# An attention and gMLP block on one core: the order written out for the first loads, batch 0 and the last two output tiles

## The chip, the cores and the metric

The kernel runs on one core of one Trainium2 chip. The metric is the time of one execution on the device in microseconds; the median of three runs is given. The profile is of one execution, and its times are microseconds from the first instruction.

## The reference

Sliding-window attention with sink positions is followed by a gMLP block. Four batches, eight heads, 768 positions, head width 64; the eight heads side by side give the 512 columns of `x`.

```python
scores = scale * q @ k.T                       # scale = 1/8
keep = (pos_k < 4) | (0 <= pos_q - pos_k < 128)
a = softmax(where(keep, scores, -1e9))
x = (a @ v).transpose(0, 2, 1, 3).reshape(4, 768, 512)
h = gelu_tanh(x @ w_in)                        # 512 -> 1024
u, v = h[..., :512], h[..., 512:]
v_n = (v - mean(v)) / sqrt(var(v) + 1e-6) * g_ln
v_s = w_sg @ v_n + b_sg[:, None]               # over the 768 positions
out = x + (u * v_s) @ w_out                    # 512 -> 512
```

All inputs and the output are float32.

## The kernel before

The whole program is a list of steps written out by hand, `STEPS` (lines 20 to 68). A step is a function's name and its indices: `QK.0.2.1` calls `QK(0, 2, 1)`. The loop at line 650 calls them in this order, and nothing reorders them, so the list fixes the order on each engine's queue. An engine takes its own instructions strictly in that order and waits for each until its inputs are there and its output buffer is free. A last letter in a step names the engine: D is VectorE (DVE), A is ScalarE (ACT), P is GpSimd (POOL).

The names, in the order of the data (b is the batch, p a pair of heads, g a group of two tiles of 128 positions, t one such tile):

- `LPK.g`, `LPQ.g` (lines 239 to 247): loads of k and q of batch 0, one pair of heads in each, issued by SyncE (SP) in float32. `CPK`, `CPQ` cast them to bfloat16. `LG` loads `g_ln`, `LC` the four sink rows of v.
- `LK`, `LQ`, `LVH`, `LW`, `LWS`, `LWO` (lines 213 to 280): loads that GpSimd issues and that cast on the way: k and q of batches 1 to 3, v by halves of the heads, `w_in` by column halves (`LW.0` is the half for v, `LW.1` for u), `w_sg` by halves and `w_out`.
- `TK`, `TQ`, `EK`, `EQ`: transposes of k and q on TensorE (PE) and the copies out of PSUM. In batch 0, `TK.0.p` transposes one pair of heads with all positions; in batches 1 and 2, `TQ.b.g` takes two tiles of all heads. Batch 3 uses transposing DMAs from SP instead: `DK`, `DQ`, and `XD` for x in batches 2 and 3.
- `QK.b.p.g` (line 463): scores of a pair of heads for two tiles, into one of two PSUM buffers `sc`. With a last `.1` it first adds a mask bias by two matmuls with the identity (lines 466 to 468). `EX` is the exponential on ScalarE, `MK` sets masked entries to zero where QK had no bias: one multiply on VectorE, or two selects on GpSimd.
- `KS`, `SK`, `SX`: the same for the sink positions. `VSK`, `VSO`, `VSM` prepare the sink rows of v.
- `AV.b.p.k` (line 502) multiplies with v, `NR` divides by the row sums and writes x.
- `XT`, `XE` transpose x on TensorE. `MV`, `GV` give the v half of gelu(x w_in), `BN`, `RS`, `NM`, `Z` its normalisation; `MU`, `GU` the u half. `WT`, `WE` transpose w_sg.
- `SP` (the step, not the engine SP), `GT`, `GM`: the product over positions, the scale and bias, the product with u.
- `OU.b.t`, `RA.b.t`, `ST.b.t` (lines 630 to 641): the last product for one tile of 128 positions, four matmuls of 512 columns into a PSUM buffer `mm`; one add of x on VectorE into a buffer `ot`; one store of 256 KB by SP.
- `HM.n` puts n matmuls on zeros ahead of the next buffer that TensorE writes (line 188), `WARM` clears their operand.

Buffers are taken in turn: four PSUM buffers `mm`, two `sc`, ten `P`, six `ot`. A step that takes the next one waits until its last reader is done; for `ot` that is the store of six tiles earlier.

While batch b is in its gMLP part, batch b+1 is in its attention part, and the list weaves the two together. Only at the start (batch 0's attention) and at the end (batch 3's gMLP) does one batch run alone.

Of the kernel before, what the change touches and what calls it, by code (L numbers as in the profile page):

```python
# [17 lines left out]


STEPS = """  # L20
WARM LPK.0 FILL LPQ.0 LPK.1 LG LPQ.1 LPK.2 MASK LPQ.2 LPK.3 CPK.0.A IDEN LPQ.3 IDEN2 MASK0 HM.8 TK.0.0 CPQ.0.A
EK.0.0.A HM.1 TQ.0.0 CPK.1.D EQ.0.0.A ZERO HM.1 TK.0.1 LC CPQ.1.P QK.0.0.0.1 EK.0.1.A QK.0.0.1 LVH.0.0 EX.0.0.0
CPK.2.D TQ.0.1 EX.0.0.1 GTR EQ.0.1.D TK.0.2 QK.0.0.2 LVH.0.1 CPQ.2.A GCP.D EK.0.2.D QK.0.1.0.1 EX.0.0.2 TQ.0.2 CPK.3.D
LQ.1.0 EX.0.1.0 CPQ.3.D QK.0.1.1 TK.0.3 EQ.0.2.D EX.0.1.1 MK.0.0.1.P TQ.0.3 EK.0.3.D QK.0.1.2.1 EQ.0.3.A VSK LQ.1.1
VSO QK.0.2.0.1 EX.0.1.2 KS.0 VSM.0 SK.0.1 LW.0 MK.0.1.1.D AV.0.0.0 SX.0.1 AV.0.1.0 EX.0.2.0 QK.0.2.1 LWS.0 NR.0.0.0
AV.0.0.1 EX.0.2.1 NR.0.1.0 AV.0.1.1 LW.1 QK.0.3.0.1 NR.0.0.1 LQ.1.2 QK.0.3.1.1 MK.0.2.1.D EX.0.3.0 NR.0.1.1 MK.0.0.2.P
AV.0.2.0 EX.0.3.1 AV.0.2.1 NR.0.2.0 AV.0.3.0 SK.0.2 NR.0.2.1 QK.0.2.2 SX.0.2 QK.0.3.2 NR.0.3.0 EX.0.2.2 AV.0.3.1
AV.0.0.2 NR.0.3.1 AV.0.1.2 EX.0.3.2 MK.0.2.2.P XT.0.0 NR.0.0.2 XT.0.1 NR.0.1.2 XE.0.0.A TQ.1.0 LK.1.0 AV.0.2.2
XE.0.1.A EQ.1.0.D MV.0.0 MK.0.3.2.P NR.0.2.2 LQ.1.3 AV.0.3.2 GV.0.0 MV.0.1 LK.1.1 NR.0.3.2 BN.0.0 LWS.1 XT.0.2 LK.1.2
# [46 lines left out]
def kernel(  # L76
# [14 lines left out]
    nc = tc.nc  # L91
# [4 lines left out]
    d_model = H * Dh  # L96
# [7 lines left out]
    KU = d_half // 128  # L104
# [26 lines left out]
    mm_ring = Ring("mm", 4, [128, 512], F32, psum)  # L131
# [6 lines left out]
    x_sb = Ring("x_sb", 2, [128, NT, d_model], BF16)  # L138
# [5 lines left out]
    ot = Ring("ot", 6, [128, d_model], F32)  # L144
# [21 lines left out]
    w_out_sb = sb.tile([128, KU, d_model], BF16, name="w_out_sb")  # L166
# [10 lines left out]
    def gated(b, hf):  # L177
        return gatedT[:, slots.setdefault((b, hf), len(slots) % 3)]
# [458 lines left out]
    def RA(b, t):  # L637
        nc.vector.tensor_add(ot.new((b, t)), mm_ring["o", b, t], x_sb[b][:, t, :])  # L638
# [51 lines left out]
```

## Time and profile before

| What | Value |
|---|---|
| median of the runs shown | 157.92 us (157.89, 157.92, 160.23) |
| the profiled execution | 159.1 us, its span 157.4 us |
| TensorE matmul busy | 147.8 us |
| VectorE busy | 126.7 us |
| ScalarE busy | 98.2 us |
| GpSimd busy | 97.1 us |
| last add ends, last store is issued | 154.3 us |

The span goes from the first to the last instruction. The profiled execution takes 1.7 us more than its span, and the runs without a profile are the ones that the median is taken of. Busy times of different engines overlap. A matmul's record covers its way through the array, so matmuls that follow each other overlap in the records; the distance between their starts is what each costs: 0.216 us for 512 columns, 0.109 us for 256. DMA issues of GpSimd take its queue's time, 0.9 us for a 128 KB load and 1.4 to 1.8 us for half of v.

### The profile page before, as it was taken

How to read it: one execution, taken by the hardware profiler on the slowest of the kernel's cores; microseconds unless marked ns; L12 is line 12 of the kernel's file. 1: busy time of each engine (PE TensorE's matmuls, PEld its weight loads, DVE VectorE, ACT ScalarE, POOL GpSimd, SP SyncE). 2: the span in 40 equal slices, each digit the busy share in tenths (PEclk: the TensorE clock that was granted, in tenths of full speed). 3: DMA queues.
4: the chain of work that ended last, by engine and by line, in shares of the span. 5: the costliest groups of instructions: out<-in, count | busy, mean ns of one | idle time of the engine just before them, and what ended most of it. 6: DMA issues, size and time to landing. Idle time of an engine off the chain costs nothing.

```text
span 157.4 us, 3863 instructions
## 1 busy us (share of the span) xinstructions
PE 147.8 (94%) x1554; PEld 95.5 (61%) x1567; DVE 126.7 (81%) x301; ACT 98.2 (62%) x108; POOL 97.1 (62%) x123
## 2 busy tenths in 40 slices
PE   6779799999998999999999999999999999999990
PEld 2355567679755759658366766457566644786540
DVE  5149986899989989497999995589999958947991
ACT  3769889548995884857986857356897013690000
POOL 3069959999969999997637916904359720302300
PEclk9978999999999999999999999999999999999998
DMA  5989999999999996999999286899000577610055
GB/s 168 314 319 112 147 202 208 167 189 215 157 150 181 154 147 45 133 139 145 144 153 187 42 223 158 226 222 142 4 0 0 104 174 298 228 71 2 0 193 209
DMA packets 83034, 23.88 MB, mean 152 GB/s; under 512 B 75524, under 2 KB 79880, under 8 KB 83016
## 3 DMA queue, kind: packets, MB, share of 16 engines
q0 software_dynamic: 64608, 11.01, 94.9%
q1 hardware_dynamic: 18408, 12.62, 28.5%
q8 instruction: 12, 0.20, 0.5%
q14 instruction: 6, 0.05, 0.1%
HBM read 24.81 MB, written 6.29 MB: 198 GB/s over the span
## 4 chain that ended last, share of the span: by engine, by line
PE 73%; DVE 12%; DMA 9%; issue 1%; SPq 1%; POOL 0%; DVEq 0%
PE mm L617 17%; PE sc L597 13%; PE sc L556 13%; PE mm L634 12%; DMA v_sb<-in_v_dram 5%; PE sc L473 5%; DMA uT<-in_q_dram 4%; DVE P L485 3%; PE mm L514 3%; DVE x_sb L531 3%; DVE gtmp L622 3%; PE mm L374 3%; PE mm L518 2%; PE mm L540 2%; PE mm L521 2%
## 5 line engine op out<-in xcount | busy, mean ns | idle before, releaser
L478 ACT ACTIVATE P<-sc 128x1024 bf16<-128x1024 f32 (+1 forms) x48 | 43.4, 953 | 9.6 <-PE sc L473 9.4
L617 PE MATMUL mm<-wsgT,z 128*128 128x384 bf16 x192 | 34.2, 326 | 0.2 <-DVE x_sb L531 0.2
L617 PEld LDWEIGHTS <-z 128*128 128x128 bf16 x192 | 17.9, 98 | 11.3 <-issue 0.4
L488 POOL TENSOR_SCALAR_AFFINE_SELECT P<-P 128x512 bf16<-128x512 bf16 x20 | 14.6, 729 | 16.5 <-ACT P L478 12.3
L560 ACT ACTIVATE vt<-sc 128x1024 f32<-128x1024 f32 x12 | 12.3, 1024 | 20.0 <-PE sc L556 20.0
L622 DVE SCALAR_TENSOR_TENSOR gtmp<-mm,g_sb,b_bc 128x384 bf16<-128x384 f32 x32 | 18.9, 609 | 4.8 <-PE mm L617 4.8
L634 PE MATMUL mm<-w_out_sb,wsg_gated 128*128 128x512 bf16 x88 | 21.9, 379 | 0.6 <-DVE x_sb L531 0.2
L627 POOL TENSOR_TENSOR wsg_gated<-gtmp,uT 128x384 bf16<-128x384 bf16 x14 | 13.2, 957 | 14.9 <-DVE gtmp L622 13.6
L597 PE MATMUL sc<-xT,w_in_sb 128*128 128x256 bf16 x192 | 22.3, 273 | 0.0
L556 PE MATMUL sc<-w_in_sb,xT 128*128 128x512 bf16 x93 | 22.1, 379 | 0.2
L569 DVE BATCH_NORM_STATS2 st<-vt 128x6 f32<-128x512 f32 x24 | 15.4, 684 | 6.5 <-ACT vt L560 6.5
L597 PEld LDWEIGHTS <-w_in_sb 128*128 128x128 bf16 x192 | 18.7, 98 | 3.1
L531 DVE TENSOR_TENSOR x_sb<-mm,rcp 128x384 bf16<-128x384 f32 (+1 forms) x36 | 18.5, 513 | 1.2
L638 DVE TENSOR_TENSOR ot<-mm,x_sb 128x512 f32<-128x512 f32 x24 | 15.8, 683 | 2.0 <-PE mm L634 1.9
L514 PE MATMUL mm<-v_sb,P 128*128 128x65 bf16 x192 | 16.7, 194 | 0.7 <-DMA v_sb<-in_v_dram 0.7
L220 POOL DMA_DIRECT2D q<-in_q_dram x18 | 16.6, 936 | 0.0
L514 PEld LDWEIGHTS <-P 128*128 128x128 bf16 x192 | 14.3, 98 | 3.3 <-issue 1.1
L473 PE MATMUL sc<-qT,kT 64*128 64x128 bf16 (+1 forms) x256 | 15.3, 245 | 0.9 <-DVE kT L198 0.6
L220 POOL DMA_DIRECT2D k<-in_k_dram x18 | 16.1, 901 | 0.0
L485 DVE TENSOR_TENSOR P<-P,mask 128x768 bf16<-128x768 bf16 (+1 forms) x22 | 15.7, 729 | 0.4 <-ACT P L478 0.4
L518 PE MATMUL mm<-v_sb,P 128*128 128x65 bf16 x160 | 15.8, 194 | 0.0
L602 ACT ACTIVATE uT<-sc 128x1024 bf16<-128x1024 f32 x12 | 12.3, 1021 | 5.6 <-PE sc L597 5.5
(89 smaller groups left out, 230.9 us busy)
## 6 DMA issues: line engine op xcount, KB each, us to landing
out_dram<-ot SPq DMA_DIRECT2D x24, 256.0 KB, 2.3
v_sb<-in_v_dram POOLq DMA_DIRECT2D x8, 384.0 KB, 8.0
q<-in_q_dram POOLq DMA_DIRECT2D x18, 128.0 KB, 5.6
k<-in_k_dram POOLq DMA_DIRECT2D x18, 128.0 KB, 5.3
wsg_gated<-in_moe_w_sg_dram POOLq DMA_DIRECT2D x2, 576.0 KB, 8.4
w_in_sb<-in_moe_w_in_dram POOLq DMA_DIRECT2D x2, 512.0 KB, 9.4
uT<-in_k_dram SPq DMA_DIRECT2D x2, 384.0 KB, 3.1
uT<-in_q_dram SPq DMA_DIRECT2D x2, 384.0 KB
```

The source lines that it names most:

```text
L220: return nc.gpsimd.dma_start(out=dst.rearrange("p (h d) -> p h d", h=H), in_=heads(src, b, i))
L473: nc.tensor.matmul(sc[:, hl, c:c + 128 * ni], at(kT, b)[rows, j, p, :], at(qT, b)[rows, i:i + ni, p, :], start=not biased, stop=(not biase ...
L478: nc.scalar.activation(out=P.new((b, p, g))[:, :, 0:w], in_=sc_ring[b, p, g][:, :, 0:w], func=AF.Exp, scale=scale)
L485: nc.vector.tensor_mul(pt[:, :, 0:w], pt[:, :, 0:w], m.unsqueeze(1).to_broadcast([128, 2, w]))
L514: nc.tensor.matmul(av[:, il, hl, :], pt[:, hl, c:c + 128], vb[:, h, i, :], start=first, stop=False)
L518: nc.tensor.matmul(av[:, il, hl, :], pt[:, hl, c:c + 128], vb[:, h, i - 1, :], start=False, stop=(i < 2 and il == n - 1 and hl == 1))
L531: nc.vector.tensor_mul(x_sb.get(b)[:, i0:i0 + n, 128 * p:128 * (p + 1)].rearrange("p t (h d) -> p t h d", h=2), av[:, :, :, 0:Dh], rcp[:, ...
L556: nc.tensor.matmul(hp[:, jl, :], xT[b][:, 2 * g + jl, c, :], w_in_sb[:, c, d_half:2 * d_half], start=(c == 0), stop=(c == KD - 1))
L597: nc.tensor.matmul(hp[:, dc // 2, 256 * (dc % 2):256 * (dc % 2 + 1)], w_in_sb[:, c, 128 * dc:128 * (dc + 1)], xT[b][:, 2 * g:2 * g + 2, c, :],
L617: nc.tensor.matmul(ps[:, 0:NH], z[b][:, si, 128 * dc:128 * (dc + 1)], wsgT[:, si, NH * hf:NH * (hf + 1)], start=(si == 0), stop=(si == NT ...
L622: nc.vector.scalar_tensor_tensor(out=gtmp.new((b, hf, dc)), in0=mm_ring["g", b, hf, dc][:, 0:NH], scalar=g_sb[:, dc:dc + 1], in1=b_bc[:, N ...
L634: nc.tensor.matmul(ps, gated(b, hf)[:, dc, 128 * tl:128 * (tl + 1)], w_out_sb[:, dc, :], start=(dc == 0), stop=(dc == KU - 1))
```

## The change

The list is written in a new order and some steps go to another engine. All loads, transposes and products of before are still there. In particular:

- SP issues `LPQ.2` ahead of `LG` and `LPK.2`, and `LPQ.3` ahead of `LPK.3`.
- In batch 0, all three `QK` of pair 0 come ahead of `TK.0.1`. `CPK.1` goes from VectorE to GpSimd, `CPQ.1` from GpSimd to VectorE, `CPQ.2` from ScalarE to VectorE; some `EK`, `EQ` change places between ScalarE and VectorE.
- Biased are now QK.0.0.1, 0.0.2, 0.2.0 and 0.2.1 (four); before they were 0.0.0, 0.1.0, 0.1.2, 0.2.0, 0.3.0 and 0.3.1 (six). There are two more MK for it. `HM` has 15 matmuls instead of 10.
- On GpSimd, `LW.0` and `LWS.0` come straight behind the two `LVH` of batch 0, ahead of `LQ.1.0` and `LQ.1.1`.
- From batch 0's gMLP on, steps of all kinds stand in a new order, among them the loads of later batches, and the stores `ST.0.*` and `ST.1.*` on SP's queue.
- `OU`, `RA` and `ST` of the tiles 5 and 2 of batch 3 are replaced by `OH`, `RH` and `SH`, each twice, for 256 columns each time. `OH` with h = 1 writes into the same PSUM buffer as h = 0. In the list, `OH.3.5.1` stands ahead of `RH.3.5.0`, and `OH.3.2.1` ahead of `RH.3.2.0`.

```diff
 STEPS = """
-WARM LPK.0 FILL LPQ.0 LPK.1 LG LPQ.1 LPK.2 MASK LPQ.2 LPK.3 CPK.0.A IDEN LPQ.3 IDEN2 MASK0 HM.8 TK.0.0 CPQ.0.A
-EK.0.0.A HM.1 TQ.0.0 CPK.1.D EQ.0.0.A ZERO HM.1 TK.0.1 LC CPQ.1.P QK.0.0.0.1 EK.0.1.A QK.0.0.1 LVH.0.0 EX.0.0.0
-CPK.2.D TQ.0.1 EX.0.0.1 GTR EQ.0.1.D TK.0.2 QK.0.0.2 LVH.0.1 CPQ.2.A GCP.D EK.0.2.D QK.0.1.0.1 EX.0.0.2 TQ.0.2 CPK.3.D
-LQ.1.0 EX.0.1.0 CPQ.3.D QK.0.1.1 TK.0.3 EQ.0.2.D EX.0.1.1 MK.0.0.1.P TQ.0.3 EK.0.3.D QK.0.1.2.1 EQ.0.3.A VSK LQ.1.1
-VSO QK.0.2.0.1 EX.0.1.2 KS.0 VSM.0 SK.0.1 LW.0 MK.0.1.1.D AV.0.0.0 SX.0.1 AV.0.1.0 EX.0.2.0 QK.0.2.1 LWS.0 NR.0.0.0
-AV.0.0.1 EX.0.2.1 NR.0.1.0 AV.0.1.1 LW.1 QK.0.3.0.1 NR.0.0.1 LQ.1.2 QK.0.3.1.1 MK.0.2.1.D EX.0.3.0 NR.0.1.1 MK.0.0.2.P
-AV.0.2.0 EX.0.3.1 AV.0.2.1 NR.0.2.0 AV.0.3.0 SK.0.2 NR.0.2.1 QK.0.2.2 SX.0.2 QK.0.3.2 NR.0.3.0 EX.0.2.2 AV.0.3.1
-AV.0.0.2 NR.0.3.1 AV.0.1.2 EX.0.3.2 MK.0.2.2.P XT.0.0 NR.0.0.2 XT.0.1 NR.0.1.2 XE.0.0.A TQ.1.0 LK.1.0 AV.0.2.2
-XE.0.1.A EQ.1.0.D MV.0.0 MK.0.3.2.P NR.0.2.2 LQ.1.3 AV.0.3.2 GV.0.0 MV.0.1 LK.1.1 NR.0.3.2 BN.0.0 LWS.1 XT.0.2 LK.1.2
-GV.0.1 WT.0 XE.0.2.D WT.1 LK.1.3 WT.2 VSM.1 MV.0.2 LQ.1.4 VSM.2 BN.0.1 LQ.1.5 MU.0.0 GV.0.2 LB.P BN.0.2 RS.0.1 MU.0.1
-GU.0.0 LQ.2.0 NM.0.1 WE.0.D WE.1.A RS.0.2 WE.2.D TK.1.0 GU.0.1 LQ.2.1 NM.0.2 MU.0.2 Z.0.0.D Z.0.1.D Z.0.4.A LK.1.4
-EK.1.0.D Z.0.5.D LK.1.5 TQ.1.1 GU.0.2 WT.3 EQ.1.1.D LK.2.0 WT.4 TK.1.1 KS.1 Z.0.2.D Z.0.3.A LVH.1.0 QK.1.0.0 WE.3.D
-QK.1.1.0 SP.0.0.0 EK.1.1.D WE.4.D SP.0.0.1 LK.2.1 EX.1.0.0 EX.1.1.0 MK.1.0.0.D LWO WT.5 TQ.1.2 GT.0.0.0 WE.5.A
-QK.1.0.1 MK.1.1.0.D QK.1.1.1 EX.1.0.1 GT.0.0.1 SP.0.0.2 GM.0.0.1.P EX.1.1.1 SP.0.0.3 GT.0.0.2 LVH.1.1 EQ.1.2.A
-GM.0.0.2.D QK.1.2.0 GT.0.0.3 QK.1.2.1 SP.0.1.0 EX.1.2.0 GM.0.0.3.D LK.2.2 GM.0.0.0.D EX.1.2.1 QK.1.3.0 GT.0.1.0 LK.2.3
-SK.1.0 EX.1.3.0 MK.1.1.1.D TK.1.2 LQ.2.2 SP.0.1.1 MK.1.2.0.D SX.1.0 EK.1.2.D GM.0.1.0.P TQ.2.0 GT.0.1.1 QK.1.0.2
-LQ.2.3 QK.1.3.1 MK.1.0.1.D EX.1.0.2 SP.0.1.2 MK.1.2.1.D LQ.3.0 EX.1.3.1 EQ.2.0.D AV.1.0.0 AV.1.1.0 MK.1.0.2.P GT.0.1.2
-TK.2.0 NR.1.0.0 QK.1.1.2 EK.2.0.A QK.1.2.2 LVH.3.0 AV.1.0.1 MK.1.3.0.D EX.1.1.2 NR.1.1.0 OU.0.0 NR.1.0.1 MK.1.3.1.P
-EX.1.2.2 OU.0.1 RA.0.0 QK.1.3.2 MK.1.1.2.P RA.0.1 QK.2.0.0 EX.1.3.2 AV.1.2.0 AV.1.3.0 NR.1.2.0 SP.0.1.3 MK.1.2.2.P
...
-QK.3.1.0 EX.3.0.0 AV.2.0.1 MK.2.2.2.P GT.1.1.1 XD.2.0 SP.1.1.2 EX.3.1.0 NR.2.0.1 AV.2.1.1 MK.3.1.0.D ST.0.0 GM.1.1.0.D
-QK.2.3.2 ST.0.1 GM.1.0.3.D QK.3.0.1 EX.2.3.2 ST.0.2 GT.1.1.2 AV.2.2.1 NR.2.1.1 OU.1.0 EX.3.0.1 MK.2.3.2.D SK.3.0
-NR.2.2.1 MK.3.0.1.P QK.3.2.0 AV.2.3.1 EX.3.2.0 SP.1.1.3 NR.2.3.1 SX.3.0 MU.2.0 XD.2.1 GT.1.1.3 RA.1.0 GM.1.1.3.P
-ST.1.0 OU.1.1 GM.1.1.2.P GU.2.0 OU.1.2 GM.1.1.1.P RA.1.1 MV.2.0 ST.1.1 LK.3.4 RA.1.2 ST.0.3 ST.0.4 MK.3.0.0.D LK.3.5
-ST.0.5 MK.3.2.0.D AV.3.0.0 LVH.3.1 GV.2.0 MV.2.1 BN.2.0 MV.2.2 GV.2.1 BN.2.1 MU.2.2 GV.2.2 BN.2.2 RS.2.1 MU.2.1 GU.2.2
...
-GT.3.1.2 OU.3.0 GM.3.1.2.P GT.3.1.3 OU.3.1 GM.3.1.3.D RA.3.0 OU.3.3 RA.3.1 ST.3.0 OU.3.4 ST.3.1 RA.3.3 OU.3.5 ST.3.3
-RA.3.4 OU.3.2 ST.3.4 RA.3.5 ST.3.5 RA.3.2 ST.3.2
+WARM LPK.0 FILL LPQ.0 IDEN LPK.1 LPQ.1 LPQ.2 LG IDEN2 MASK LPK.2 LPQ.3 CPK.0.A MASK0 LPK.3 HM.8 TK.0.0 CPQ.0.A
+EK.0.0.D HM.1 TQ.0.0 ZERO EQ.0.0.A HM.3 QK.0.0.0 CPK.1.P QK.0.0.1.1 EX.0.0.0 LVH.0.0 EX.0.0.1 MK.0.0.0.D QK.0.0.2.1
+CPQ.1.D TK.0.1 EX.0.0.2 LC CPQ.2.D VSK TQ.0.1 LVH.0.1 EK.0.1.D TQ.0.2 EQ.0.1.A EQ.0.2.A HM.1 QK.0.1.0 LW.0 QK.0.1.1
+CPQ.3.D EX.0.1.0 LWS.0 CPK.2.D EX.0.1.1 HM.2 TQ.0.3 CPK.3.D LQ.1.0 TK.0.2 EQ.0.3.D TK.0.3 EK.0.2.A LQ.1.1 QK.0.1.2
+EK.0.3.D GTR EX.0.1.2 QK.0.2.0.1 VSO KS.0 VSM.0 EX.0.2.0 SK.0.2 MK.0.1.2.P SK.0.1 MK.0.1.0.D QK.0.3.0 GCP.A AV.0.0.0
+EX.0.3.0 AV.0.1.0 NR.0.0.0 LW.1 QK.0.2.1.1 SX.0.1 MK.0.3.0.D SX.0.2 QK.0.3.1 NR.0.1.0 EX.0.2.1 MK.0.1.1.P AV.0.2.0
+AV.0.3.0 AV.0.0.1 NR.0.2.0 AV.0.0.2 EX.0.3.1 NR.0.3.0 QK.0.2.2 AV.0.1.1 NR.0.0.1 EX.0.2.2 XT.0.0 MK.0.3.1.P NR.0.0.2
+QK.0.3.2 XE.0.0.A NR.0.1.1 AV.0.2.1 MK.0.2.2.P AV.0.1.2 NR.0.2.1 AV.0.3.1 EX.0.3.2 MV.0.0 NR.0.1.2 LK.1.0 NR.0.3.1
+MK.0.3.2.D LQ.1.2 AV.0.2.2 GV.0.0 AV.0.3.2 LK.1.1 NR.0.2.2 XT.0.1 NR.0.3.2 WT.0 LQ.1.3 XE.0.1.A TQ.1.0 WE.0.D XT.0.2
+EQ.1.0.D LK.1.2 MV.0.1 XE.0.2.D LK.1.3 BN.0.0 LWS.1 MV.0.2 GV.0.1 LK.2.0 BN.0.1 LB.P WT.1 GV.0.2 MU.0.1 WE.1.A BN.0.2
+RS.0.1 TQ.1.1 GU.0.1 LK.1.4 TK.1.0 NM.0.1 MU.0.0 EK.1.0.D Z.0.0.A RS.0.2 LQ.1.4 NM.0.2 Z.0.1.D Z.0.2.A EQ.1.1.D
+Z.0.4.A MU.0.2 LQ.1.5 VSM.1 GU.0.0 LK.1.5 Z.0.3.D WT.2 LQ.2.0 GU.0.2 WT.3 WE.2.D TK.1.1 LK.2.1 Z.0.5.D QK.1.0.0
+QK.1.1.0 WE.3.D WT.4 LQ.2.1 EK.1.1.D SP.0.0.0 EX.1.0.0 KS.1 LQ.2.2 SP.0.0.1 EX.1.1.0 GT.0.0.0 LVH.1.0 WE.4.A QK.1.0.1
+GT.0.0.1 QK.1.1.1 EX.1.0.1 TQ.1.2 LVH.1.1 WT.5 SP.0.0.2 EX.1.1.1 EQ.1.2.A QK.1.2.0 LWO GT.0.0.2 QK.1.3.0 SP.0.0.3
+GM.0.0.0.D WE.5.A LQ.2.3 MK.1.0.1.D TK.1.2 EX.1.2.0 MK.1.1.0.D LQ.2.4 SP.0.1.0 GM.0.0.1.D EX.1.3.0 GT.0.0.3 LQ.3.0
+MK.1.1.1.D EK.1.2.A QK.1.2.1 QK.1.3.1 MK.1.2.0.D GM.0.0.3.P SK.1.0 MK.1.0.0.D TK.2.0 SX.1.0 LQ.3.1 GT.0.1.0 SP.0.1.1
+EX.1.2.1 EK.2.0.D TQ.2.0 EX.1.3.1 GT.0.1.1 MK.1.2.1.P AV.1.0.0 MK.1.3.0.D AV.1.1.0 EQ.2.0.A GM.0.0.2.D QK.1.0.2
+MK.1.3.1.P NR.1.0.0 QK.1.1.2 SP.0.1.2 EX.1.0.2 NR.1.1.0 LQ.3.2 SP.0.1.3 EX.1.1.2 GT.0.1.2 MK.1.0.2.D AV.1.2.0 GT.0.1.3
+AV.1.3.0 MK.1.1.2.P QK.1.2.2 NR.1.2.0 QK.1.3.2 EX.1.2.2 OU.0.0 NR.1.3.0 LQ.3.3 EX.1.3.2 OU.0.1 RA.0.0 MK.1.2.2.P
+AV.1.0.1 ST.0.0 RA.0.1 AV.1.1.1 LK.2.2 MK.1.3.2.D XT.1.0 NR.1.0.1 LQ.2.5 AV.1.2.1 XE.1.0.A NR.1.1.1 QK.2.0.0 LVH.2.0
...
+MK.2.2.0.D SP.1.0.0 SX.2.0 RA.0.5 DK.3.0 EX.2.0.1 SP.1.0.1 GT.1.0.0 MK.2.0.1.P OU.0.2 GT.1.0.1 QK.2.1.1 QK.2.2.1
+MK.2.2.2.P EX.2.3.2 ST.0.3 MK.2.3.1.D SP.1.1.2 ST.0.4 ST.0.5 MK.2.3.0.D GM.1.1.0.P GT.1.1.1 QK.3.0.0 QK.3.1.0 EX.3.0.0
+AV.2.3.0 GM.1.0.2.D MK.2.3.2.P GT.1.1.2 AV.2.0.1 EX.3.1.0 NR.2.3.0 AV.2.1.1 GM.1.0.3.P AV.2.2.1 NR.2.0.1 XD.2.0
+AV.2.3.1 NR.2.1.1 SK.3.0 NR.2.2.1 QK.3.2.0 SX.3.0 QK.3.0.1 OU.1.0 EX.3.0.1 NR.2.3.1 OU.1.1 XD.2.1 EX.3.2.0 SP.1.1.3
+ST.0.1 OU.1.2 GT.1.1.3 RA.1.0 MV.2.0 GM.1.1.3.P MK.3.0.0.D ST.1.0 GM.1.1.1.P ST.0.2 MU.2.0 GM.1.1.2.P GV.2.0 LVH.3.1
+RA.1.1 RA.1.2 MV.2.1 ST.1.1 GU.2.0 MK.3.0.1.D LK.3.4 BN.2.0 LK.3.5 AV.3.0.0 GV.2.1 MV.2.2 NR.3.0.0 BN.2.1 MU.2.2
...
+SP.3.1.2 GM.3.0.3.D GT.3.1.1 SP.3.1.3 GM.3.1.1.P GT.3.1.2 OU.3.0 GT.3.1.3 OU.3.1 GM.3.1.3.D GM.3.1.2.D RA.3.0 OU.3.3
+RA.3.1 ST.3.0 OU.3.4 RA.3.3 ST.3.1 OH.3.5.0 ST.3.3 RA.3.4 OH.3.5.1 RH.3.5.0 OH.3.2.0 ST.3.4 RH.3.5.1 SH.3.5.0 OH.3.2.1
+RH.3.2.0 SH.3.5.1 RH.3.2.1 SH.3.2.0 SH.3.2.1
 """
...
+    def cols(h):
+        return slice(d_model // 2 * h, d_model // 2 * (h + 1))
+
+    def OH(b, t, h):
+        hf, tl = t // 3, t % 3
+        ps = mm_ring["o", b, t] if h else fresh(mm_ring, ("o", b, t))
+        for dc in range(KU):
+            nc.tensor.matmul(ps[:, cols(h)], gated(b, hf)[:, dc, 128 * tl:128 * (tl + 1)],
+                             w_out_sb[:, dc, cols(h)], start=(dc == 0), stop=(dc == KU - 1))
+
+    def RH(b, t, h):
+        nc.vector.tensor_add(ot.get((b, t))[:, cols(h)], mm_ring["o", b, t][:, cols(h)], x_sb[b][:, t, cols(h)])
+
+    def SH(b, t, h):
+        nc.sync.dma_start(out=out[b, 128 * t:128 * (t + 1), cols(h)], in_=ot[b, t][:, cols(h)])
+
+        KS, SK, SX, QK, EX, MK, AV, NR, XT, XE, XD, MV, GV, BN, RS, NM, Z, MU, GU, WT, WE, SP, GT, GM, OU, RA, ST, OH, RH, SH)}
```

## The prediction

> **What bounds the kernel now.** I read the page first, for the share of each engine and the granted clock.
>
> ```profile
> span 157.4 us, 3863 instructions
> ...
> PE 147.8 (94%) x1554; PEld 95.5 (61%) x1567; DVE 126.7 (81%) x301; ACT 98.2 (62%) x108; POOL 97.1 (62%) x123
> ...
> PEclk9978999999999999999999999999999999999998
> ```
>
> TensorE is busy 94% of the span, so what a new order can win lies in the few stretches where it isn't. The table by stretches shows them (PE busy first, PEclk after POOL).
>
> ```profile
> 6.36:9.77 3.41, 1.65 (x29) 0.85 (x27) 0.87 (x5) 1.30 (x3) 0.40 (x1) 1.00 1.03 379
> 9.77:13.18 3.41, 3.41 (x44) 2.27 (x43) 2.29 (x4) 3.08 (x5) 3.41 (x3) 0.50 0.61 170
> ...
> 16.60:20.00 3.40, 2.46 (x49) 1.72 (x48) 3.19 (x10) 2.72 (x4) 3.40 (x5) 1.00 3.44 147
> ```
>
> ```profile
> 36.00:47.50 11.50, 11.50 (x130) 8.39 (x128) 10.35 (x22) 10.97 (x14) 10.17 (x11) 1.00 2.21 175
> 47.50:56.00 8.50, 7.66 (x110) 5.32 (x111) 8.22 (x15) 6.18 (x8) 8.50 (x11) 1.00 2.15 168
> ...
> 83.00:95.00 12.00, 11.78 (x175) 7.78 (x175) 11.54 (x30) 8.65 (x11) 7.80 (x12) 1.00 0.69 160
> 95.00:124.00 29.00, 28.89 (x289) 18.69 (x291) 24.50 (x55) 18.62 (x19) 17.07 (x22) 1.00 0.74 109
> ```
>
> Idle TensorE time sits at the start (1.76 us of the first 3.41 us shown, 0.94 us of the third) and at 47.5 to 56 (0.84 us), where VectorE has 8.22 of 8.50 us. From 56 on almost none is left. Then the chain that ended last, for what sets the start, the middle and the end:
>
> ```profile
> 9.37 0.79 POOL q L202
> 10.15 7.94 DMA v_sb<-in_v_dram
> ...
> 48.33 1.48 DVE P L485 x2
> ...
> 153.60 0.69 DVE ot L638
> ```
>
> At the start v is last: GpSimd can issue it only after its cast of the second q pair, and it lands 7.94 us later. In the middle it is VectorE's mask work. At the end one add and one store follow the last matmul. The timeline gives the first exponential:
>
> ```profile
> 6.77 0.80 ACT L197 COPY qT<-mm 128x768 bf16<-128x768 bf16 x1 [0.30 <-PE mm L368]
> 8.20 0.56 DVE L198 CAST k<-uT 128x768 bf16<-128x768 f32 x1 [3.74 <-DMA uT<-in_k_dram]
> 10.22 1.73 ACT L478 ACTIVATE P<-sc 128x768 bf16<-128x768 f32 x2
> ```
>
> The third pair load (k of pair 1) is only there at 8.20, and before stands TK.0.1, which waits for it, ahead of the first QK; so pair 0, complete at 7.57, waits as well.
>
> **The start, step by step.** (a) After the change all three QK of pair 0 stand ahead of TK.0.1. qT of pair 0 ends at 7.57 as now. kT's copy moves to VectorE, where such a copy takes 0.95 us against 0.80, and ends near 6.6, still first. HM.3 puts three warm matmuls in front (0.22 us each by the 512-wide spacing, 0.43 at the pace of the first ones), to 7.4 or 8.0. With four QK matmuls the first EX begins at about 8.1 instead of 10.22.
>
> (b) From there ScalarE sets the start. Its spacings in the trace are 0.91 us for an EX of 1024, 0.70 for 768 and for a transposed copy, 0.30 for SX, 0.91 for XE. Up to the last EX of batch 0 it has 8 and 4 EX (10.1), EQ.0.1, EQ.0.2 and EK.0.2 (2.1), GCP (0.2), two SX (0.6) and XE.0.0 (0.9): 13.9 us. Following the queues against each other I find waits of about 2.0 us: 0.5 until the transposes of pair 1 are through (Q1 is there at 9.28), 0.4 for TK.0.2, 0.2 for QK.0.1.2, 0.7 for QK.0.3.0, which stands on PE behind SK.0.2 and so behind KS.0 on VectorE, 0.2 elsewhere. 8.1 + 13.9 + 2.0 = 24.0. A table load (1.28), GV.0.0 (0.92) and XE.0.1 (1.02), which now stands behind it, bring 27.2; with 0.4 us for hand-overs MV.0.1 starts at 27.6. Before, the same step started at 27.91, with XT.0.2 (0.45) and WT.0 (0.34) still to be done; after, they lie in front of it. The lead is 0.3 + 0.8 = 1.1 us. With waits of 1.0 or 3.0 us it is 2.1 or 0.1, and these are my bounds.
>
> (c) PE itself has two biased QK fewer (two 384-wide matmuls at 0.16 or 512-wide at 0.22 us each: 0.7 us saved) and five warm matmuls more (1.1 us at 0.22). The warm ones stand where PE waits for (a) and the casts; without that cover they cost 0.4 us net, inside the bounds. The unmasked QK need two more MK: one 0.65 us on VectorE and 1.2 on GpSimd, on engines that (b) leaves time.
>
> (d) The loads. The cast that GpSimd makes first is now k of pair 1, at 8.20, not q at 9.37. So LVH.0.0 is issued at 9.03 instead of 10.15 and with the same 7.9 us lands near 16.9 instead of 18.05. Then come VSK (0.4 us), the second v, w_in, w_sg and only then LQ.1.0 and LQ.1.1. From issues and times to landing, v's second half lands at 20.8 in the trace, the two q loads at 21.3 and 22.1, w_in at 24.6 and w_sg at 27.3: 2.5 to 2.7 us for each big transfer, 0.5 to 0.8 for a q load. In the new order, 1.1 us sooner, that makes w_in 22.2, w_sg 24.9 and LQ.1.1 26.2. By the walk PE reaches MV.0.0 (needs w_in) at 23.4, WT.0 at 26.3 and TQ.1.0 (needs LQ.1.1) at 26.6. The cover for moving w_in and w_sg up is 0.4 us thin. Later in the queue LVH.1.0 has two more 128 KB loads in front (1.7 us) and the 1.1 us lead: from 47.7 to 48.3, where AV.1.0.0 ran at 52.3 before. LWO moves behind LVH.1.1, to about 53.6; OU.0.0 needs it at about 55. No stall there.
>
> **The middle.** Between 36 and 57 VectorE loses WE.4 (0.54), EK.1.2 (0.67), MK.1.2.1 (0.82) and EQ.2.0 (0.68) and gets MK.1.0.2 (0.82) and EK.2.0 (0.67): 1.2 us less. ScalarE gets WE.4 and EK.1.2 (0.8 + 1.0) and is what is late next: it is busy 10.97 of 11.50 us up to 47.5, but idle for 1.73, 0.59 and 0.77 us behind that. The gain can't pass PE's idle 0.84 us and is zero if ScalarE's 1.8 us reach the QKs; I take 0.6.
>
> **Batches 2 and 3.** PE is full, so the moved MK, GM, EK and Z steps can't win, only lose. On SP, ST.0.0 stands ahead of DK.3.0, ST.0.3 to ST.0.5 ahead of XD.2.0, ST.0.1 and ST.0.2 behind XD.2.1. RA.1.1 needs ST.0.1's buffer: XD.2.1's issue (up to 2.13), the store's (0.33) and its landing (2.3) make 4.8 us after the last NR of batch 2. On PE, SK, QK.3.2.0, QK.3.0.1, three OU and one SP (0.33 + 0.5 + 2.6 + 1.0 = 4.4) come before RA.1.1 could run, and MV.2.0 (1.73) covers the rest. I take 0, bounds -0.3 and +0.8 (one such stall of VectorE uncovered, in the stretch 83 to 95 where it is busy 11.54 of 12).
>
> **The tail.** OU, RA and ST of tiles 5 and 2 become two halves each. Four 512-wide matmuls at 0.216 are eight 256-wide at 0.109: nothing. In the built order both matmul halves of a tile stand ahead of its first add, and that add's wait counts the last matmul of the second half; the second add waits for nothing from PE. So no add starts sooner. The last step becomes two adds of 0.42 (the 128x256 row of NR, from PSUM like these) instead of one of 0.69: 0.15 later. Stores of 256 KB land 2.0 to 2.7 us after issue; the half may land as late as these, or, bounding by bytes alone, half the time sooner for the spread of 0.7, 0.35. Sum -0.2 to +0.15; I take 0. The Trainium skill (DMA: Bandwidth & Descriptors, Anatomy of one DMA) gives 2.0 us plus bytes over 436 GB/s, for the GpSimd path; as an estimate from that page 128 KB less save 0.3 us and the tail would be -0.15; the 2.0 us floor of the trace agrees.
>
> **Sum.** -1.1 - 0.6 + 0 + 0 = -1.7: span 157.4 to 155.7. The profiled execution took 159.1 with its span, so it would take 157.4; the median shown is 157.92, 1.2 under the profiled one, and with the same difference I get 156.2. The ends of the terms add up to -3.4 and +0.9.
>
> **Rivals.** *A, the forecast:* 156.2.
>
> *B, the lead is swallowed:* TQ.1.0 meets the late LQ.1.1, or the waits on ScalarE are 3 us. If LVH.0.0 isn't sooner, LQ.1.1 lands at 27.3 or later and PE stands 0.7 us with everything behind TQ.1.0; lead 0.4, middle 0.3: 157.2. For it: 0.4 us of cover. Against: two queues have to agree on being late.
>
> *C, more than forecast:* waits of 1.0 us at the start (-2.1), the whole 0.84 in the middle, -0.2 and more behind: 154.6. For it: PE's clock falls to 0.50 in the second window above and the new order keeps PE busier before it. Against: ScalarE's queue, not PE, sets (b).
>
> *D, slower:* the half clock moves to where PE is the bound. In the trace a window with 1.65 us of PE is followed by one at 0.50, of the same 3.41 us, and it cost little, since v was waited for. The new order has thin PE work from 9.8 to 13.2 (three transposes, two QK, one warm matmul, about 2.5 us). If that decides, the windows 13.2 to 20 run at half pace; each costs up to 1.7 us (half of 3.41), and of the 3.4 some 0.7 lies beside ScalarE: -1.7 + 2.7 = +1.0, 158.9. Against: 2.5 is more than 1.65. The Trainium skill (TensorE: Matmul & The Clock Gate, Part 1) says that the gate watches a free-running window of 3413 ns and halves the clock after an idle one; the 3.41 us of the trace agree, and by it the outcome may change from run to run.
>
> *E, the halves do overlap* (the first add runs during the second half's matmuls): the end is 0.27 for the shorter last add and up to 0.35 for the store sooner: 155.6. The built order speaks against it.
>
> **How the numbers follow.** A 0.43, B 0.19, C 0.20, D 0.13, E 0.05. The time is A's. The range takes in C's 154.6 with the last tenths to the lower end of the terms and D's 158.9: 154.2 to 158.9, leaving 0.2 out. 2%, about what a measurement of this kernel can tell from no change, is 3.2 us, so faster means under 154.8: most of C, 0.19. Slower means over 161.1: D with more than two windows, 0.06. Within: 0.75.
>
> **What would show it.** Right: the first EX near 8.1, LVH.0.0 landing near 17, MV.0.1 near 27.6 with XT.0.2 and WT.0 done, PE idle well under 0.84 us in the stretch before OU.0.0, two adds after the last matmul. Wrong: a wait of TQ.1.0 or MV.0.0 on a DMA (B), a clock of 0.50 after 13 us (D), an add between the halves' matmuls (E), new VectorE or DMA waits of PE after 56.

## The result, and the profile after

The changed kernel takes 160.29 us (median of 160.12 to 160.56) against 157.9 us before: ratio 1.015, 95% interval 1.011 to 1.019. That is 1.5% slower, and outside the forecast's range of 154.2 to 158.9. Ratios and their intervals leave out executions more than 1.5% above the fastest of the same kernel, which takes most executions of before with a stretch at half clock out of them.

The page after:

```profile
span 158.4 us, 3910 instructions
...
PE 147.8 (93%) x1576; PEld 95.4 (60%) x1576; DVE 130.6 (82%) x302; ACT 98.0 (62%) x109; POOL 102.4 (65%) x124
...
PEclk9999999999999999999999999999999999999999
```

VectorE is busy 3.9 us longer than before, GpSimd 5.3, and no slice is at half clock. The table by stretches, as before (PE busy first, then PEld, DVE, ACT, POOL, PEclk):

```profile
6.36:9.77 3.41, 3.24 (x39) 1.42 (x35) 1.46 (x6) 2.73 (x4) 1.39 (x2) 1.00 1.04 370
9.77:13.18 3.41, 2.38 (x47) 1.39 (x41) 3.05 (x4) 2.71 (x4) 3.33 (x4) 1.00 1.08 231
16.60:20.00 3.40, 2.44 (x42) 1.20 (x40) 3.32 (x11) 2.65 (x7) 2.86 (x4) 1.00 2.48 171
36.00:47.50 11.50, 11.50 (x129) 8.21 (x128) 8.34 (x18) 11.31 (x15) 11.50 (x13) 1.00 2.19 168
47.50:56.00 8.50, 8.50 (x124) 6.01 (x124) 8.35 (x17) 7.33 (x10) 8.48 (x11) 1.00 2.27 164
83.00:95.00 12.00, 10.72 (x166) 7.16 (x165) 11.62 (x26) 7.20 (x9) 10.10 (x13) 1.00 0.84 155
95.00:124.00 29.00, 29.00 (x280) 18.43 (x279) 24.80 (x55) 17.99 (x19) 18.61 (x22) 1.00 0.74 114
```

The start (6.36 to 9.77) and 47.5 to 56 are fuller, as forecast, and from 36 to 47.5 VectorE has 2 us less to do. New is 83 to 95: 1.28 us without a matmul, where before had 0.22. TensorE's waits around there (us in total, times, longest) in the changed kernel and in before, and the chain of the changed kernel:

```profile
PE mm L515 <- DVE P L486: 1.2, 1, 1.2
```

```profile
PE mm L617 <- DVE x_sb L531: 0.2, 1, 0.2
```

```profile
85.31 0.53 DVE gtmp L623
85.83 0.60 DVE v_sink L350
...
88.35 1.81 DVE P L486 x2
90.16 0.05 issue
90.21 0.27 PE mm L515 x3
```

AV.2.3.0 waits for MK.2.3.1 and MK.2.3.0, which VectorE does last, one behind the other.

The first trace of before turned out to be a bad base. Another trace of the same kernel (b0_before_again below) has this page, and this cast and first exponential:

```profile
span 156.3 us, 3876 instructions
...
PEclk9999999999999999999999999999999999999999
```

```profile
7.10 0.56 DVE L198 CAST k<-uT 128x768 bf16<-128x768 f32 x1 [2.64 <-DMA uT<-in_k_dram]
...
8.99 1.73 ACT L478 ACTIVATE P<-sc 128x768 bf16<-128x768 f32 x2
```

The cast that waits for the "late" pair load ends its wait at 7.10, not 8.20, the first EX is at 8.99, not 10.22, and no window is at 0.50. So I compare with this trace too.

**A ledger.** At any time take the start of the latest matmul and add the cost of all matmuls still to come, each at its usual spacing in full stretches (137.2 us in all for before, 137.7 after, with five warm matmuls more and two biased QK fewer). This projected end rises only when TensorE loses time, so orders can be compared at any point. Some traces lack a few matmul records (the first of before 13 of 1567); what they cost is counted at their place in the order.

| Projected end of the matmuls (us) | before, first trace | before, again | after | after, again |
|---|---|---|---|---|
| at 36 us | 145.9 | 144.8 | 145.4 | 144.8 |
| at 72 us | 148.9 | 147.8 | 147.9 | 148.6 |
| at 96 us | 151.8 | 150.7 | 151.9 | 152.6 |
| at the end | 153.4 | 152.3 | 153.6 | 154.4 |
| last matmul's start to span's end | 4.2 | 4.2 | 4.9 | 4.9 |

Against before at full clock the changed kernel is 0.6 us behind at 36 us, level at 72, 1.4 behind at the end of the matmuls, and the tail adds 0.7: 2.1, the difference of the spans (158.4 and 156.3).

### The profile page after: what moved, and what is told of

Read it like the earlier page. It is cut to its first block, busy times and chain, and to the rows that moved or that the text cites. A ratio compares the mean times of both kernels' runs of the same rounds, so it can differ in the third digit from the quotient of the medians.

```text
span 158.4 us, 3910 instructions
## 1 busy us (share of the span) xinstructions
PE 147.8 (93%) x1576; PEld 95.4 (60%) x1576; DVE 130.6 (82%) x302; ACT 98.0 (62%) x109; POOL 102.4 (65%) x124
## 4 chain that ended last, share of the span: by engine, by line
PE 47%; DVE 17%; issue 2%; DVEq 0%
PE mm L618 10%; PE sc L598 10%; PE sc L557 10%; PE mm L635 9%; DVE P L486 4%; DVE x_sb L532 4%; DVE gtmp L623 4%; PE sc L474 2%; PE mm L375 1%; DVE ot L639 1%; PE mm L648 1%; DVE wsg_gated L628 1%; PE mm L515 1%; DVE rcp L531 1%; PE mm L519 1%
## 5 line engine op out<-in xcount | busy, mean ns | idle before, releaser
L623 DVE SCALAR_TENSOR_TENSOR gtmp<-mm,g_sb,b_bc 128x384 bf16<-128x384 f32 x32 | 19.6, 613 | 8.9 <-PE mm L618 8.6
L628 POOL TENSOR_TENSOR wsg_gated<-gtmp,uT 128x384 bf16<-128x384 bf16 x17 | 16.5, 984 | 12.1 <-DVE gtmp L623 12.1
L635 PE MATMUL mm<-w_out_sb,wsg_gated 128*128 128x512 bf16 x88 | 21.0, 379 | 0.0
L486 DVE TENSOR_TENSOR P<-P,mask 128x768 bf16<-128x768 bf16 (+1 forms) x25 | 18.7, 765 | 2.2 <-ACT P L479 2.2
L515 PE MATMUL mm<-v_sb,P 128*128 128x65 bf16 x192 | 16.2, 194 | 2.2 <-DVE P L486 1.8
L579 POOL TENSOR_TENSOR rs<-rs,neg_half 128x4 f32<-128x4 f32 (+1 forms) x8 | 7.4, 928 | 16.4 <-DVE rs L574 14.9
L639 DVE TENSOR_TENSOR ot<-mm,x_sb 128x512 f32<-128x512 f32 x22 | 14.7, 682 | 2.7 <-DMA out_dram<-ot 1.5
L519 PE MATMUL mm<-v_sb,P 128*128 128x65 bf16 x160 | 15.4, 194 | 0.0
```

The costliest lines, as they stand in the source:

```text
L486: nc.vector.tensor_mul(pt[:, :, 0:w], pt[:, :, 0:w], m.unsqueeze(1).to_broadcast([128, 2, w]))
L515: nc.tensor.matmul(av[:, il, hl, :], pt[:, hl, c:c + 128], vb[:, h, i, :], start=first, stop=False)
L519: nc.tensor.matmul(av[:, il, hl, :], pt[:, hl, c:c + 128], vb[:, h, i - 1, :], start=False, stop=(i < 2 and il == n - 1 and hl == 1))
L623: nc.vector.scalar_tensor_tensor(out=gtmp.new((b, hf, dc)), in0=mm_ring["g", b, hf, dc][:, 0:NH], scalar=g_sb[:, dc:dc + 1], in1=b_bc[:, N ...
L628: (nc.vector if e == "D" else nc.gpsimd).tensor_mul(gated(b, hf)[:, dc, :], gtmp[b, hf, dc], uT[b][:, dc, NH * hf:NH * (hf + 1)])
L635: nc.tensor.matmul(ps, gated(b, hf)[:, dc, 128 * tl:128 * (tl + 1)], w_out_sb[:, dc, :], start=(dc == 0), stop=(dc == KU - 1))
```

## The experiments

Theory 1: the changed order of batch 2 costs through VectorE between 81 and 91 us, and the halves cost in the tail through their stores. Theory 2: the lead at the start was measured against a disturbed trace. Rivals stand with each run. Time ratios are against before, run beside each kernel.

### The base: before again, and the late pair load

**b0_before_again**: no edit. **a0_after_again**: the changed kernel, no edit.

> The kernel before as it is, for another trace. Theory 2 (the half clock at 9.8 to 13.2 us in its first trace cost about 1.5 us and is absent from most executions): a trace without 0.50 in it has a span of about 156 us, and the projected end of its matmul work at 36 us is 1 to 1.5 us sooner than in the first trace, at or below that of the changed kernel. Theory 1 of the prediction (the half clock cost little, since v was waited for): span 157 us or more also at full clock.

> The changed kernel as it is, beside the others on the same chip, and another trace of it. Theory 1: its matmul work ends at about the same time from trace to trace, within 0.4 us, since the waits on VectorE at 52 to 60 and 88.8 us swallow what the start varies by; 160.3. Rival (the whole kernel varies with its start): projected ends 0.9 us apart.

b0: full clock, span 156.3, projected end at 36 us 1.1 us sooner than in the first trace. Theory 2 holds. a0: 160.88 us, ratio 1.017 (1.012 to 1.022); its median span, 159.2, is 2.8 us above that of before at full clock beside it (156.4). Its start was 0.6 us earlier, but it lost that and more at 52 to 60 us and ended 0.7 us later; my 0.4 us for the variation was too tight. The step that differs most between the two traces there is the mask MK.1.3.0 on VectorE, in the first trace of the changed kernel and in a0:

```profile
50.58 1.13 DVE L486 TENSOR_TENSOR P<-P,mask 128x768 bf16<-128x768 bf16 x1
```

```profile
50.02 2.81 DVE L486 TENSOR_TENSOR P<-P,mask 128x768 bf16<-128x768 bf16 x1
```

In both GpSimd starts a select 0.03 us ahead of it. In the first the mask is done beside the second select of four; in a0 it ends only behind all four, and TensorE then waits for the NR behind it. Of eight traces with this order up to batch 1, a0 and e2 (below) show the 2.81 us. No run tests what decides.

**g5_pair_load_late** issues that load later:

```diff
-... LPK.1 LG LPQ.1 LPK.2
+... LG LPQ.1 LPK.1 LPK.2
```

> The kernel before with one load moved: LPK.1 (k of pair 1) issued behind LPQ.1, 0.9 us later, so that it lands as late as it did in the first trace of before. Theory 2 (that trace was slower since this load came late: TensorE idles in one 3.4 us window and runs the next at half clock): first EX near 9.9 to 10.2 us, a clock of 0.50 for one window of 3.4 us in most executions, spans 157.3 to 158.7; executions without it 156 to 156.5. Rival (the half clock has nothing to do with the load): as often as with before itself, one in three, and spans as before.

All 4 executions have a granted clock of 0.978 to 0.988 and spans of 157.1 to 158.1; 159.14 us, 1.011 (1.007 to 1.014). The first EX came at 11.32, later than expected. Its table for the first two clock windows:

```profile
6.30:9.71 3.41, 1.11 (x24) 0.72 (x25) 0.66 (x2) 1.17 (x2) 0.83 (x1) 1.00 1.04 383
9.71:13.13 3.42, 3.42 (x45) 2.12 (x41) 1.32 (x5) 2.61 (x4) 3.21 (x3) 0.50 0.80 182
```

A window with 1.11 us of TensorE is followed by one at half clock, as one with 1.65 us was in the first trace of before. The windows with 2.71 us of b0 and with 2.49 us of after were not. The Trainium skill (TensorE: Matmul & The Clock Gate, Part 1) speaks of an idle window ahead of the half clock; here it needs no idle one. The busy time alone doesn't decide either: in e5 (below) a window with 1.58 us was followed by one at half clock, in e6 one with 1.50 us (65.64 to 69.05 us) and in e3 one with 1.80 us were not.

**h4_warm_before_pair1** fills that window in the kernel before:

```diff
-... ZERO HM.1 TK.0.1 ...
+... ZERO HM.5 TK.0.1 ...
```

> The kernel before with five warm matmuls instead of one ahead of TK.0.1, where TensorE waits for the pair load. Theory 2 (the half clock follows a window of 3.4 us in which TensorE has too little to do while that load is late): no execution with a clock of 0.98 to 0.99, median 157.4 to 157.9 and no runs of 159 to 160. Rival (0.9 us more of warm matmuls delay pair 1's transposes and cost as much): every run 0.3 to 0.9 us longer.

Median 157.83 us against 158.22 of before beside it. All 10 executions are at 0.994 or more. Of the 31 of before, 11 had 0.978 to 0.989 with a median span of 158.2; the other 20 have 156.1, as h4 has. The ratio, 0.996 (0.992 to 1.0005), includes 1. So what is shown is that the half clock is gone, and not a faster undisturbed run.

### The start and the middle by themselves

**e4_start_of_after** takes the changed order up to Z.0.5 (38 us), the rest as before; **e5_after_to_batch1** up to the last NR of batch 1 (59 us); **e6_late_part_of_after** the reverse, before up to MU.1.0 and then the change.

> The changed order up to Z.0.5 (batch 0's attention, its loads, the first normalisations; about 38 us), then all steps that are left in the order of before, with the tail of before. Theory 1 (in the profiled runs the projected end of the matmul work is 0.5 us earlier at 36 us, and before's later order keeps what it is given): 0.5 us faster than before, 157.4. Theory 2 (the 3.4 us at half clock in the profiled run of before are not in its other runs, and are what the profiled run is 1.2 us longer by): before is really 0.7 us ahead at 36 us, and this kernel is about 0.7 us slower than before, 158.6. Rival: the later order of before swallows the lead, 157.9.

> The changed order up to the last NR of batch 1 (about 59 us), then what is left in the order of before, tail of before. Theory 1 (projected end of the matmul work 1.1 to 1.7 us earlier at 56 to 64 us, lost only later, between 59 and 92 us, in the changed order of batch 2): 1.1 us faster than before, 156.8. Theory 2 (1.2 us of that is before's half clock in the profiled run alone): about as before, 157.9. Rival (the lead is lost in any order of batch 2, because VectorE bounds 83 to 95 us): 157.6 to 157.9 with a wait of PE on VectorE's masks near 84 to 92 us.

> The order of before up to MU.1.0 of batch 1 (about 59 us), then all that is left in the order of the change, with the column halves at the end. Theory 1 (the changed order of batches 2 and 3 has waits of its own between 84 and 92 us, about 1.0 us against before's order, and the tail halves cost 0.7 to 0.95 us): 1.7 to 2 us slower than before, 160. If only the tail costs: 0.9 us slower, 159.2. If the start is what costs: as before, 158.3.

e4: 158.8 us, 1.004 (1.000 to 1.009), nothing won. At full clock its median span is 157.0 against 156.0 of before, so it loses 1.0 us; its trace, with 156.5, is one of its faster executions. There the projected end at 36 us is 144.6, hardly better than b0's 144.8, and then TensorE meets a wait for the copy of kT that is longer than in before (0.6 us at this place in b0):

```profile
PE sc L473 <- DVE kT L198: 1.3, 1, 1.3
```

e5 (167.3 us) and e6 (165.6) don't answer the question. Joined in the middle, the two orders leave a load of batch 2 too late in GpSimd's queue, and both have TensorE waiting for it at 63 to 72 us:

```profile
PE mm L374 <- DMA k<-in_k_dram: 4.8, 1, 4.8
```

```profile
PE mm L374 <- DMA q<-in_q_dram: 3.4, 2, 2.2
```

They show only that these two orders can't be joined here. From 72 us on e6's trace loses 6.0 us where b0 loses 4.4.

### Batch 2: one mask

**e3_mask_early** moves one step of the changed kernel:

```diff
-... SP.1.1.2 ST.0.4 ST.0.5 MK.2.3.0.D ...
+... SP.1.0.2 RA.0.2 MK.2.3.0.D EX.2.2.1 ...
```

> The changed kernel with one step moved: MK.2.3.0 (a mask on VectorE) from behind MK.2.3.1 to right behind RA.0.2, where VectorE idles 0.7 us. Theory 1 (PE stands 1.34 us at 88.8 us for two masks of VectorE, back to back behind VSM.3, two NR and a GT): the wait falls to about 0.4 us and the kernel is 0.9 us faster than the changed one, 159.4. Rival (VectorE bounds the whole stretch, and any order of its work ends at the same time): the wait moves behind, gain under 0.3 us, 160.

159.79 us, 1.1 less than a0 beside it. TensorE's 1.2 us wait is gone, and the ledger loses 4.9 us from 72 us to the end instead of 5.75. The rival, that it would move behind, is wrong.

**g1_mask_early_whole_tail**: by a slip the mask stood behind VSM.3 and not behind RA.0.2; the tail is that of before. **h1_mask_at_ra_whole_tail** is the intended kernel, **h2_and_vsm2_early** has VSM.2 behind VSM.1 as well.

> The changed kernel with MK.2.3.0 behind RA.0.2 (as in e3_mask_early) and the tail of before (whole tiles). Theory 1 (one wait of 1.35 us on VectorE's masks and 0.85 us of tail are nearly all that the change costs): both add up, 0.85 + 0.85 = 1.7 us faster than the changed kernel, span 156.7, within 0.7 us of an undisturbed run of before. Rival (start or middle cost as well): 1 us or more behind before still.

> The changed kernel with MK.2.3.0 right behind RA.0.2 and the tail of before; in g1_mask_early_whole_tail the mask had slipped to the place behind VSM.3, 4.4 us later, where VectorE has no gap. Theory 1 (VectorE is the bound from 81 to 91 us, and a mask taken out of this stretch gives 1 us back): projected end of the matmul work 0.8 us or more sooner than in g1 at an equal start, span 156.2 to 156.8, time about 158.2, within 0.5 us of before. Rival (the end of that stretch is set by something else and the place of the mask doesn't matter): as g1, 158.9.

> As h1, and VSM.2 (0.68 us of VectorE) goes back to batch 0, behind VSM.1, about where before has it. Theory 1: VectorE's stretch before 91 us is 0.6 us shorter again, span 0.3 to 0.6 us less than h1, level with an undisturbed run of before or ahead of it, 157.5 to 157.9. Rival (VSM.2 lies in one of VectorE's gaps at 79 to 82 us and costs nothing): as h1.

The slip made a good test. The same mask in e3 and in g1 (timeline of VectorE), and GpSimd beside it in g1:

```profile
81.14 0.55 DVE L486 TENSOR_TENSOR P<-P,mask 128x768 bf16<-128x768 bf16 x1
```

```profile
85.51 0.99 DVE L485 TENSOR_TENSOR P<-P,mask 128x768 bf16<-128x768 bf16 x1
```

```profile
84.96 1.12 POOL L491 TENSOR_SCALAR_AFFINE_SELECT P<-P 128x512 bf16<-128x512 bf16 x1
```

At 81 us VectorE had a gap and GpSimd was idle: 0.55 us. At 85.5 VectorE had no gap and GpSimd was selecting: 0.99 us, and TensorE waited three times for VectorE, behind 86.4, 88.9 and 90.6 us (0.5, 0.3 and 0.3 us), instead of once. g1 lost 5.75 us from 72 us on, exactly as the changed kernel does, although it was 0.9 us ahead at 72: the end of this stretch is VectorE's. h1 and h2 lost 4.9, as e3 did.

g1 158.91 us, 1.010 (1.007 to 1.013); h1 158.91, 1.002 (0.997 to 1.007); h2 158.90, 1.004 (1.000 to 1.008). By the ledger h1 gains 0.8 us on g1 from 72 us on, as expected, but it started 0.7 us later and the medians are equal, on two chips; against before at full clock beside each, g1's median span is 1.4 us longer and h1's 1.1. VSM.2 costs nothing, so the rival of h2 holds. At full clock the median spans of h1 and h2 are 157.2 against 156.1 of before. Their traces, against b0, are 0.6 and 0.4 us behind at 36 us, win 0.6 up to 72, lose 0.5 after it (4.9 against 4.4 to 4.5 in the six traces that keep the order of before up to the last tiles; not broken down further) and 0.5 and 0.3 in the tail.

### The tail

**e1_halves_on_before** and **e2_whole_on_after** change tails: `OH`, `RH`, `SH` of the tiles 5 and 2 in before, `OU`, `RA`, `ST` in the changed kernel. **h3_half_adds_one_store** halves products and adds in before, but stores whole tiles. **g4a_halves_two_queues** is e1 with the second half of each stored by ScalarE; **g4b_halves_overlapped** puts each add ahead of the next half's matmuls as well.

```diff
-    nc.sync.dma_start(out=out[...cols(h)], in_=ot[b, t][:, cols(h)])
+    (nc.scalar if h else nc.sync).dma_start(out=out[...cols(h)], in_=ot[b, t][:, cols(h)])
```

> The kernel before with only its last two tiles (5 and 2 of batch 3) added and stored in column halves, in the order of the change; all else as before. Theory 1 (two more store issues stand one behind the other on SP behind the last adds, so the last store is issued 0.85 us later and lands 0.7 to 0.9 us later): 0.7 to 0.95 us slower than before, about 158.7. The prediction's step (tail costs nothing): 157.9, within 0.2 of before. Rival E (halves overlap): 0.6 us faster, 157.3.

> The changed kernel with the tail of before: tiles 5 and 2 of batch 3 whole, one add and one 256 KB store each. Theory 1: 0.7 to 0.95 us faster than the changed kernel, about 159.4, still 1.5 us slower than before in time. If the tail costs nothing: 160.3. If the tail were all of the difference: 157.9.

> The kernel before with the matmuls and adds of its two last tiles in halves, but one store of 256 KB for each. Theory 1 (it is the number of stores that costs: SP issues them one by one, and the end waits for each of their semaphores): last matmul to the end of the span 4.2 to 4.4 us, as before, against 4.9 with four stores; time within 0.2 us of before. Rival (halved matmuls and adds cost): 4.8, 0.6 us slower.

> The kernel before with the two last tiles in column halves in the change's order, but the second half of each is stored from ScalarE's queue. Theory 1 (the halves cost 0.85 us since four store issues of 0.35 to 0.5 us stand behind each other on SP): about 0.1 to 0.2 us behind before, time from the last matmul to the end of the span near 4.0 us and not 4.8. Rival (halved adds and 128 KB stores of 1 KB rows are what costs): 0.85 us as with one queue, 4.8.

> As g4a, and each half's add now stands in the list ahead of the next half's matmuls, so that it waits for its own four matmuls alone. Theory 1: the last add shrinks from 0.69 to 0.42 us and starts right behind the last matmul, the last store is half as big: 0.3 to 0.5 us faster than before, 157.5 to 158. Rival (the adds in PSUM delay the matmuls of the other half in the same buffer, or the store's time does not fall with its size): 0 to 0.2 us of either sign.

| | time, ratio to before | median span at full clock, less that of before | last matmul to the end |
|---|---|---|---|
| e1, four half stores on SP | 159.46, 1.008 (1.003 to 1.012) | 0.8 | no trace to use (376 us) |
| e2, change with whole tiles | 161.1, 1.018 (1.012 to 1.024) | 3.1 | 4.5 |
| h3, half adds, one store | 158.45, 1.002 (0.998 to 1.007) | 0.2 | 4.2 |
| g4a, two queues | 158.01, 1.002 (0.998 to 1.005) | 0.5 | 4.7 |
| g4b, adds in between | 159.76, 1.016 (1.008 to 1.023) | 1.7 | 4.3 (matmuls end later) |

Full clock means a mean granted clock of 0.99 or more. Halved products and adds cost next to nothing (h3); four stores do (e1). With a second queue the ratio can't be told from 1 (g4a), but the tail of its trace is 0.5 us longer than in before. The half stores of the changed kernel, by their source line, and the whole stores of b0:

```profile
L655 SPq DMA_DIRECT2D out_dram<-ot x4: 332/354/496, 153.4 to 155.2; - x4
```

```profile
L641 SPq DMA_DIRECT2D out_dram<-ot x24: 332/424/873, 90.5 to 153.2; - x24
```

In after the chain ends with the adds,

```profile
153.83 0.42 DVE ot L652
154.26 0.33 DVEq L702
```

the last add ends at 154.59 and the last store is issued at 155.17, 0.59 us later, since SP issues four in a row; in b0 that is 0.03. The half lands 1.90 us after its issue, the whole 2.11. From that landing to the end it is 1.35 us instead of 0.99: SP waits for each DMA semaphore in turn, 0.06 to 0.07 us apart, and that of the last store is in the third of ten waits, where in b0 it was in the eighth of nine. 0.56 - 0.21 + 0.36 - 0.04 (the last add ends a little sooner) = 0.67.

In g4a the last store is issued 0.03 us after the last add, and all half stores land in 1.8 to 1.9 us:

```profile
DMA to landing us min/median/max: 1.8/1.8/1.9
```

Its tail is 4.7 and not the 4.0 expected, since the span goes on for 1.80 us behind that landing. The last store's semaphore is now the first DMA's that SP waits for; all the other waits follow it, and with them a pause of 0.47 us, which in b0 (0.46 us) is over before the last store lands. What the pause is, stays open.

e2 did not gain in time. Its tail is 0.4 us shorter, but its trace has the mask of 2.81 us, and by the ledger it loses 1.1 us more between 36 and 72 us than the first trace of the change. In the traces of e2, g1, h1 and h2 whole tails take 4.5 to 4.7, not 4.2: the last store lands 2.4 to 2.6 us after issue. In these four an instruction fetch of 8 KB starts 0.8 to 1.0 us after that issue; in before, b0 and h3, where the store lands in 2.1 us, it starts 1.6 to 1.8 us after it. That fits, but no run tests it.

In g4b the adds wait for four matmuls only, but the next half's matmuls then wait for the add:

```profile
PE mm L647 <- DVE ot L651: 1.2, 2, 0.7
```

Both halves are in one PSUM buffer. The Trainium skill (PSUM — Partial Sum Buffer, PSUM bank collisions raise a hardware error) has TensorE and VectorE kept apart by bank and not by address. The waits of g4b agree; by that rule rival E could not come true with one buffer, whatever the order.

## Why the prediction was wrong, by its own steps

- **The base.** "The profiled execution took 159.1 ... with the same difference I get 156.2": this step failed first. Every execution on record takes 1.7 us more than its span, profiled or not, so the 1.2 us between profile and median were that execution's own late load and half clock, and the change has neither. Taking the 1.2 off and also measuring the start against that execution counts the same stall twice. From 158.0 (span 156.3 and the same 1.7) the same steps give 156.3; what was measured is 2.4 us above before. Against b0 the terms -1.1, -0.6, 0 and 0 came out as +0.6, -0.6, +1.3 and +0.7.
- **The start, -1.1.** The walk was nearly right: first EX 7.78 (8.1 said), LVH.0.0 issued 9.16 (9.03), MV.0.1 at 28.11 with XT.0.2 and WT.0 done (27.6). Its counterpart was wrong. At full clock MV.0.1 of before starts at 26.62, where the first trace has 27.75 (the chain's 27.91). With the 0.8 us for XT.0.2 and WT.0 that is 27.4, 0.2 us ahead even of the walk's 27.6. In eight traces at full clock with the changed start the projected end at 36 us is 144.5 to 145.4 (median 145.0), in five with the start of before at full clock 144.2 to 144.9 (144.8). The lead is -0.2, not +1.1. "It cost little, since v was waited for" is the sentence that hid it: in b0, without the half clock and the late load, the same work ends 1.1 us sooner.
- **Warm matmuls** (c): they were to cost 0.4 us net without cover. The ledger has 0.55 us more TensorE work, since the biased QK are fewer but three of the four left are 512 wide. How much of it was covered, no run shows.
- **The middle, -0.6.** From 36 to 72 us the changed kernel loses 2.5 us, b0 3.1: -0.6 as said, and 0.5 to 0.7 less than b0 in e3, g1, h1 and h2. PE idles 0.00 us in 47.5 to 56. In a0 and e2 the mask of 2.81 us turned it into a loss of 0.7 and 0.5 us.
- **Batches 2 and 3, 0 (to +0.8).** Mis-sized, and the wrong instance was named. "One such stall of VectorE uncovered, in the stretch 83 to 95" did happen, for the masks of pair 3, and with it a sign of being wrong that was named, a new VectorE wait of PE after 56. With what follows it is 5.75 against 4.4 us, +1.3: 0.8 for the place of one mask, the other 0.5 not broken down. The wait that I followed, RA.1.1 for its store, is there (1.5 us of VectorE) and TensorE didn't feel it. I counted how many masks VectorE has and not what stands in front of each.
- **The tail, 0.** The sum had the adds (+0.15 said, -0.04 measured) and the landing (0 to -0.35 said, -0.21 measured). It had nothing for two more issues on SP (+0.56) and for the place of the last semaphore in SP's closing waits (+0.36): +0.7.
- **Rivals.** D had the sign and not the mechanism: the clock is 1.00 throughout. B's waits for LQ.1.1 and w_in didn't occur. A and C share the bad base.

## What to carry to other kernels

Before a gain is worked out from one trace, hold its span against the other executions: a low mean clock (0.987 here) and a window at 0.50 say that its stalls may not be those of the median. In an order written by hand, ask of each moved step what its engine does in the microseconds before its reader needs it, and what the neighbour does; a mask in a gap was worth 0.8 us against the same mask 4 us later. Splitting a last store costs an issue for each part, and its place among the closing waits; a second queue took over the issue but not the waits (g4a).

## What was not expected of the hardware

- A clock window with 1.1 or 1.65 us of matmuls in 3.41 us was followed by one at half clock. Together with the late load before it that costs 2 us of span (156.1 to 158.2). With four more warm matmuls (0.9 us) it came in none of 10 executions. One window with 1.50 us (e6) was not followed by half clock.
- A 768-wide mask on VectorE took 0.54 to 0.56 us in all 63 cases in these traces in which GpSimd was idle. Of 31 that had GpSimd's selects beside them for at least 30% of their time, 22 took 0.98 us or more, two of them 2.81; the nine others, all the same step in the order of before, took 0.55.
- A whole-tile store lands 2.1 us after its issue in one order and 2.4 to 2.6 us in another, with the same instructions at the end.
